# A new order for the first sequence's steps, its sums in the tiles of the weights

## The chip, the cores and the metric

The kernel runs on one core of one Trainium2 chip. The metric is the device time of one execution in microseconds (us), the median of several; lower is better.

## What is computed

A batch of two sequences (3008 x 256 each) goes through a circular convolution along the sequence, done as an FFT, a product with a filter and an inverse FFT, and then through two dense layers with their own activations:

```python
X = np.fft.rfft(x, axis=1)
y = np.fft.irfft(X * (filt_r + 1j * filt_i), n=3008, axis=1)   # 2 x 3008 x 256
h = y.reshape(6016, 256) @ moe_w_in                            # 256 -> 2048
g = np.where(h > 0, h, np.exp(np.minimum(h, 0)) - 1)
z = g @ moe_w_out                                              # 2048 -> 256
h = z @ moe2_w_in
out = (h * np.clip(h + 3, 0, 6) / 6) @ moe2_w_out
```

## The kernel before

3008 is 47 x 64, so each transform is done as two stages of small matrix products. The 256 channels are worked as two halves h = 0, 1. For the first sequence a half goes through these steps, each named by a letter, the half and a number in a string of tokens, `PROLOGUE`, which is walked once in order (line 1042). Each token issues its instructions on the engines' queues, and every engine works its queue strictly in that order.

- **A** (`s1t`): first stage, seven groups of up to five products; one copy of the bank into the tile `zt` (line 79 on ScalarE, line 81 on VectorE). Those of half 0 are done ahead of the string.
- **T** (`tr`): four transposes (line 173) and one copy, six per half. **S** (`s2_mm`, then `mult`): the second stage's product (line 204), then on VectorE three products with the filter, straight from PSUM (line 216 twice on 64 rows, line 217 once), and on GpSimd one sum of the two results into a tile `ws` (line 219).
- **F** (`f_sign`, line 149): GpSimd changes signs in the imaginary part of one filter tile, once it is loaded. `mult` of the same (h, g) needs it. Two are issued ahead of the string, ten by tokens.
- **I** (`i2_mm`, `i2_evac`): the inverse second stage's product from `ws` (line 224), a ScalarE copy (line 234), a store to DRAM (line 235). **V**: four loads of a half's stores (line 239). **O** and **o** (`i1_mm`, `i1_evac`): the inverse first stage (line 247) with its copies on ScalarE (O) or VectorE (o).
- **x, b, M, B** load, split and transform the beginning of the second sequence's half 0 (its first stage, lines 88 to 90 with the tile `s_h`); **X** splits results into high and low parts (lines 84 and 85); **G** and **H** are the first products of the first dense layer.
- **w** loads a weight tile; **c** and **k** make one step each in the conversion of weights: seven steps for the first tile (c), twelve for the next ones (k). The steps are: |w| on ScalarE (line 297), two scalings on VectorE (lines 299, 300), one each of lines 304, 306 and 308 on VectorE, a ScalarE copy with the difference of line 316, and the sum of line 318. The first k of a tile also issues the load of a raw tile two tiles on.

After the string a loop over units of the first layer follows, whose VectorE work per unit is line 500, line 85 and further conversion steps.

All loads and stores named here are issued by SyncE in the order of the program; the filter tiles are loaded ahead of the string, in an order of their own (`LOADS`). A PSUM bank (seven rotate) is given to the next product that asks, in the order in which the banks are given up, so step n waits for the copy or the products of the step seven places ahead of it. In SBUF, tiles of 2 KB per partition come from `p2` (20 of them), the weights' tiles from `wpool` (16 of 4 KB).

Of the kernel before, what the change touches and what calls it, by code (L numbers as in the profile page):

```python
# [9 lines left out]
F32 = mybir.dt.float32  # L10
# [13 lines left out]
P = 128  # L24
# [23 lines left out]
def fft_conv_moe_moe2(ctx, tc, xp, fq, sg, cs1, cs1t, cs2, ci2, ci1, ident, w1i, w1o, w2i, w2o, out):  # L48
    nc = tc.nc
    const = ctx.enter_context(tc.tile_pool(name="const", bufs=1))  # L50
    wpool = ctx.enter_context(tc.tile_pool(name="wpool", bufs=16))
# [9 lines left out]
    def name(s):  # L61
        uid[0] += 1
        return f"{s}_{uid[0]}"
# [4 lines left out]
    def t2(shape, dt=F32):  # L68
        return p2.tile(shape, dt, tag="t2", name=name("t2"))

    def bank():
        return ps.tile([P, 512], F32, tag="ps", name=name("ps"))
# [4 lines left out]
    def evac(eng, dst, src):  # L77
        if eng is nc.scalar:
            nc.scalar.activation(dst, src, AF.Copy)
        else:  # L80
            eng.tensor_copy(dst, src)  # L81
# [10 lines left out]
    def flat(t):  # L92
        return t.rearrange("p k d -> p (k d)")
# [4 lines left out]
    def sorted_(t, k=2):  # L98
        return t.rearrange("p (b a) -> p a b", a=k)
# [13 lines left out]
    def load_mat(key, src, queue=nc.scalar):  # L113
        k, m = src.shape
        mats[key] = const.tile([k, m], F32, name=key)
        queue.dma_start(mats[key], src)
# [17 lines left out]
    xin, filt, zs, ws, vin, accs, yblk = {}, {}, {}, {}, {}, {}, {}  # L134
# [7 lines left out]
    def f_load(b, h, g):  # L142
        filt[b, h, g] = t4([P, 2, 4, P])
        nc.sync.dma_start(filt[b, h, g], fq[h, g])
# [9 lines left out]
    def s1t(b, h, jg, eng):  # L154
        if jg == 0:
            zt[h] = p12.tile([P, NK2, 2, 2, NJ], F32, tag="zt", name=name("zt"))
        acc = bank()
        j0, n = jg * TG, min(TG, NJ - jg * TG)
        for j in range(j0, j0 + n):
            nc.tensor.matmul(  # L160
                acc[:, (j - j0) * KP : (j - j0 + 1) * KP], xin[b, h, j // 8][:KP, j % 8, :],
                mats["s1t"][:KP], start=True, stop=True,
            )
        evac(
            eng,
            zt[h].rearrange("p k c h j -> p (c h) k j")[:, :, :, j0 : j0 + n],
            acc[:, : n * KP].rearrange("p (j c k) -> p c k j", j=n, c=4),
        )

    def tr(b, h, g, eng):  # L170
        acc = bank()
        for k in range(4):
            nc.tensor.transpose(
                acc[:, k * P : (k + 1) * P],
                zt[h][:, 4 * g + k].rearrange("p c h j -> p (c h j)"), mats["id"],
            )
        zs[b, h, g] = t2([P, 512])
        evac(eng, zs[b, h, g], acc)
# [29 lines left out]
    def mult(b, h, g):  # L208
        f = filt.pop((b, h, g))
        acc, parted = accs.pop((h, g)), lambda t: t  # L210
        if b:
            acc, parted = sorted_(acc), halves_of
        u, v = t2([P, 512]), t2([P, 512])
        for c in range(2):
            a, o = slice(64 * c, 64 * c + 64), slice(64 - 64 * c, 128 - 64 * c)
            nc.vector.tensor_tensor(out=parted(v[o]), in0=acc[a], in1=parted(flat(f[a, 1])), op=ALU.mult)
        nc.vector.tensor_tensor(out=parted(u), in0=acc, in1=parted(flat(f[:, 0])), op=ALU.mult)
        ws[b, h, g] = t2([P, 512])
        nc.gpsimd.tensor_tensor(out=ws[b, h, g], in0=u, in1=v, op=ALU.add)

    def i2_mm(b, h, g, parts=None):
# [622 lines left out]
    def fetch1(f):  # L844
# [9 lines left out]


    PROLOGUE = """
        T00 T01 T02 S00 T03 F01 S01 T04 F01 S02 T05 F01 S03 I00 F01 S04 I01 F01 A10 A11 F01
        S05 I02 A12 A13 A14 I03 F01 A15 A16 I04 T10 c01 T11 c01 w00 I05 F01 x00 x01 V00 T12
        S10 T13 S11 T14 F01 S12 T15 S13 I10 F01 S14 I11 S15 I12 O00 I13 b00 c01 O01 I14 c01
        b01 o02 O03 I15 M00 c01 b02 V10 c01 X00 O04 w01 b03 c01 X01 k02 O05 O06 X02 k02 B00  # L860
        B01 B02 B03 G00 G01 k03 O10 o11 G02 X10 o12 X11 O13 X12 o14 k02 H00 H01 k02 O15 k01
        H02 O16
    """
    LOADS = [(0, None, q, None) for q in range(4)]
    for x in "F00 F01 F02 F03 X0 X1 X2 X3 F04 F05 F10 W0 M F11 F12 F13 F14 F15".split():
# [150 lines left out]
    with tc.manual_schedule():  # L1016
        for key, src in (("s1t", cs1t), ("id", ident), ("sg", sg), ("s2", cs2), ("i2", ci2), ("i1", ci1)):
            load_mat(key, src)
        three = const.tile([P, 1], F32, name="three")
        nc.vector.memset(three, 3.0)  # L1020
        engs = (nc.scalar, nc.vector)

        acc = bank()
        for n in WARM:
            zeros = (nc.const_aps.tensor(0.0, [P, k], F32) for k in (P, n))
            nc.tensor.matmul(acc[:, :n], *zeros, start=True, stop=True)
        for h, g, q, r in LOADS:
            if q is not None:
                x_load(0, h, q)
            elif g is not None:  # L1030
                f_load(0, h, g)
            elif r is not None:
                w_raw(0, r)
            else:
                load_mat("s1", cs1, nc.sync)
        for jg in range(JG):
            s1t(0, 0, jg, engs[jg % 2])
        lead = w_chain(0, WLEAD, lambda f: None)
        f_sign(0, 0, 0)
        f_sign(0, 0, 1)  # L1040
        nsign = 2
        for step in PROLOGUE.split():
            what, h, g = step[:-2], int(step[-2]), int(step[-1])
            if what == "T":
                tr(0, h, g, nc.scalar if g > 1 else engs[g])
            elif what == "S":
                s2_mm(0, h, g)
                mult(0, h, g)
            elif what == "A":
                s1t(0, h, g, engs[g % 2])  # L1050
            elif what == "I":
                i2_mm(0, h, g)
                i2_evac(0, h, g)
            elif what == "V":
                for q in range(4):
                    v_load(0, h, q)
            elif what == "O":
                i1_mm(0, h, g)
                i1_evac(0, h, g, nc.scalar)
            elif what == "o":  # L1060
                i1_mm(0, h, g)
                i1_evac(0, h, g, nc.vector)
            elif what == "k":
                steps(conv, g)
            elif what == "c":
                steps(lead, g)
            elif what == "X":
                x_split(0, g, h)
            elif what == "F":
                for _ in range(g):  # L1070
                    f_sign(0, *divmod(nsign, 6))
                    nsign += 1
            elif what == "x":
                x_load(1, h, g)
            elif what == "w":
                w_raw(0, WLEAD + g)
            elif what == "b":
                s1_split(h, g)
            elif what == "B":
                s1_mm(1, h, g, parts.pop(("x", h, g)))  # L1080
                s1_evac(1, h, g)
            elif what == "G":
                g1_half(units[g], 0)
            elif what == "H":
                g1(units[g])
                if g:
                    g_split(units[g - 1])
            elif what == "M":
                split_mat("s1")

        for n, u in enumerate(units):
            place[0] = n
            for fn in pre[n]:
                fn()
            if n >= NI:
                g1(u)
                g_split(units[n - 1])
            if n >= SKEW:
                g2(units[n - SKEW])
            for fn in post[n]:  # L1100
                fn()
        def rest(n):
            def run():
                if n == NU:
                    g_split(units[-1])
                g2(units[n - SKEW])
                for fn in post[n]:
                    fn()
            return run

        old = None
        n = place[0] = NU
        for l, p in ROUNDS:
            for q in range(GROUPS):
                old = group(l, p, q, old, [rest(NU + i) for i in range(3)], pre[n : n + 4])
                n += 4
        prod(old.l, old.p, old.q, 3, old.c, False)
        old.high((1, 1))
        old.gate((1, 0))
        old.add((0, 1), old.u2, old.c)  # L1120
        old.low((1, 1))
        old.high((1, 0))
        old.relu((0, 1))
        old.low((1, 0))
        old.gate((0, 1))
        old.high((0, 1))
        old.low((0, 1))
        for key in ((0, 0), (1, 1), (1, 0), (0, 1)):
            old.second(key)
            if key == (1, 0):  # L1130
                out_evac(old.l, old.p, 0)
        out_evac(old.l, old.p, 1, True)
# [82 lines left out]
```

## Time and profile before

| | us |
|---|---|
| median of 3 runs | 1050.47 (1050.16 to 1052.39) |
| the profiled execution | 1050.34 |
| its span, first to last instruction | 1048.6 |
| PE busy | 1037.6 |
| VectorE (DVE) busy | 876.6 |
| ScalarE (ACT) busy | 807.0 |
| GpSimd (POOL) busy | 198.6 |

The span is cut by the profile into rows of instructions with start, duration and the idle time ahead of them. PE is the matrix engine, PEld its weight loads, SPq the issues of SyncE. The ends of matrix products are modelled, so the times between starts tell more than the busy share: a product of lines 204 and 224 takes 0.86 between starts (two instructions), a group of ten on lines 160 or 247 takes 1.11, and one product of lines 88 to 90 with 512 columns takes 0.216.

### The profile page before, as it was taken

The numbers are of one execution on the slowest core, as the hardware profiler recorded it, in microseconds if no ns is written. First come the engines' busy times: TensorE is split into PE (matmuls) and PEld (weight loads), VectorE is DVE, ScalarE is ACT, GpSimd is POOL, SyncE is SP. The second block draws the span as 40 slices with busy tenths as digits, with TensorE's granted clock in tenths as the row PEclk, the third lists the DMA queues.
The fourth block names the chain that finished last, engine by engine and source line by source line (L and its number), as shares of the span: only waits on it lengthen the run. The fifth ranks groups of instructions, "written<-read, shape, count | busy, mean of one in ns | idle before, by whom it ended". The sixth has DMA issues, their size and how long they took to land.

```text
span 1048.6 us, 14397 instructions
## 1 busy us (share of the span) xinstructions
PE 1037.6 (99%) x5022; PEld 913.1 (87%) x5022; DVE 876.6 (84%) x1412; ACT 807.0 (77%) x1453; POOL 198.6 (19%) x215
## 2 busy tenths in 40 slices
PE   8999999999999999999999999999999999999998
PEld 6688888888899889988888888888888888888998
DVE  4799999788877988788988988888888888887776
ACT  3488887897788888888988877777777777777766
POOL 3700001355437943200111100010010010000000
PEclk9999999999999999999999999999999999999999
DMA  9983100475536634510474531100100100100101
GB/s 263 330 280 124 46 1 1 143 228 176 167 125 213 220 128 141 178 41 1 161 261 132 209 121 41 41 21 21 41 21 21 41 18 18 41 1 1 41 1 36
DMA packets 58057, 107.32 MB, mean 102 GB/s; under 512 B 5024, under 2 KB 33696, under 8 KB 57984
## 3 DMA queue, kind: packets, MB, share of 16 engines
q1 hardware_dynamic: 52112, 88.16, 25.2%
q0 software_dynamic: 4896, 17.83, 5.2%
q8 instruction: 39, 0.64, 0.2%
q10 hardware_dynamic: 976, 0.41, 0.2%
q14 instruction: 34, 0.28, 0.1%
HBM read 69.42 MB, written 36.96 MB: 101 GB/s over the span
## 4 chain that ended last, share of the span: by engine, by line
PE 87%; DMA 4%; POOL 3%; DVE 2%; ACT 2%; issue 1%; ACTq 0%; SPq 0%; POOLq 0%; DVEq 0%
PE ps L88 26%; PE ps L90 26%; PE ps L89 26%; PE lone L90 3%; PE lone L88 3%; PE lone L89 3%; DMA t<-in_fq 2%; DMA scr<-t 1%; PE ps L247 1%; POOL t L367 1%; PE ps L224 1%; POOL t L377 1%; DMA sg<-in_sg 1%; POOL t L332 1%; POOL t L356 0%
## 5 line engine op out<-in xcount | busy, mean ns | idle before, releaser
L88 PE MATMUL ps<-t,w 128*128 128x512 f32 (+1 forms) x1072 | 403.0, 376 | 0.9 <-DVE t L500 0.8
L90 PE MATMUL ps<-t,w 128*128 128x512 f32 (+1 forms) x1072 | 401.8, 375 | 0.1
L89 PE MATMUL ps<-t,w 128*128 128x512 f32 (+1 forms) x1072 | 401.6, 375 | 0.2 <-DVE w L318 0.2
L88 PEld LDWEIGHTS ps<-t,w 128*128 128x128 f32 x1072 | 202.6, 189 | 25.6 <-DVE t L500 2.0
L90 PEld LDWEIGHTS ps<-t,w 128*128 128x128 f32 x1072 | 202.6, 189 | 25.3 <-DVE t L692 1.3
L89 PEld LDWEIGHTS ps<-t,w 128*128 128x128 f32 x1072 | 202.6, 189 | 24.9 <-DVE w L318 1.6
L692 DVE TENSOR_TENSOR t<-t,t 128x512 fp32r<-128x512 f32 (+1 forms) x256 | 175.7, 700 | 25.8 <-ACT t L687 24.3
L687 ACT ACTIVATE t<-t 128x512 fp32r<-128x512 f32 (+1 forms) x256 | 154.3, 616 | 6.4 <-DVE t L677 6.1
L641 ACT ACTIVATE t<-ps 128x512 f32<-128x512 f32 (+1 forms) x175 | 102.5, 586 | 61.5 <-PE ps L90 59.8
L661 ACT ACTIVATE t<-t,three 128x512 f32<-128x512 f32 (+1 forms) x143 | 96.5, 707 | 38.6 <-DVE t L647 37.9
L677 DVE SCALAR_TENSOR_TENSOR t<-t,t 128x512 f32<-128x512 f32 (+1 forms) x143 | 96.8, 703 | 33.3 <-ACT t L661 32.8
L497 ACT ACTIVATE t<-ps 128x512 f32<-128x512 f32 (+1 forms) x128 | 74.3, 580 | 46.9 <-PE ps L90 36.4
L647 DVE TENSOR_TENSOR t<-ps,t 128x512 f32<-128x512 f32 (+1 forms) x128 | 86.6, 677 | 11.5 <-ACT t L641 11.0
L498 ACT ACTIVATE t<-t 128x512 f32<-128x512 f32 (+1 forms) x128 | 79.3, 620 | 4.0
L500 DVE SCALAR_TENSOR_TENSOR ps<-t,ps 128x512 f32<-128x512 f32 (+1 forms) x76 | 50.4, 663 | 28.4 <-ACT t L498 27.9
L85 DVE TENSOR_TENSOR t<-t,t 128x512 fp32r<-128x512 f32 (+2 forms) x96 | 69.9, 733 | 4.2 <-ACT t L84 4.1
L84 ACT ACTIVATE t<-t 128x512 fp32r<-128x512 f32 (+2 forms) x108 | 65.2, 616 | 2.5 <-DVE t L81 2.0
L561 POOL TENSOR_TENSOR t<-t,t 128x512 f32<-128x512 f32 (+1 forms) x12 | 16.2, 1351 | 253.2 <-DVE t L647 224.0
L88 PE MATMUL ps<-t,t 128*128 128x512 f32 (+1 forms) x160 | 60.1, 376 | 0.0
L89 PE MATMUL ps<-t,t 128*128 128x512 f32 (+1 forms) x160 | 60.1, 376 | 0.0
L90 PE MATMUL ps<-t,t 128*128 128x512 f32 (+1 forms) x160 | 60.1, 376 | 0.0
L90 PE MATMUL lone<-t,w 128*128 128x512 f32 (+1 forms) x144 | 54.0, 375 | 1.0 <-DVE t L85 1.0
(118 smaller groups left out, 1612.3 us busy)
## 6 DMA issues: line engine op xcount, KB each, us to landing
t<-in_fq SPq DMA_DIRECT2D x24, 512.0 KB, 6.2
scrw<-t SPq DMA_DIRECT2D x16, 512.0 KB, 3.0
w<-scrw POOLq DMA_DIRECT2D x16, 512.0 KB, 4.3
scr<-t SPq DMA_DIRECT2D x24, 256.0 KB, 3.4
t<-scr SPq DMA_DIRECT2D x16, 384.0 KB, 5.1
t<-in_xp SPq DMA_DIRECT2D x15, 384.0 KB, 6.3
scrx<-t SPq DMA_DIRECT2D x10, 512.0 KB, 3.0
t<-scr POOLq DMA_DIRECT2D x10, 512.0 KB, 5.9
```

The costliest lines, as they stand in the source:

```text
L85: eng.tensor_tensor(out=lo, in0=src, in1=_f32(hi), op=ALU.subtract)
L88: nc.tensor.matmul(acc, wh, xh, start=start, stop=False, skip_group_check=more)
L89: nc.tensor.matmul(acc, wl, xh, start=False, stop=False, skip_group_check=more)
L90: nc.tensor.matmul(acc, wh, xl, start=False, stop=stop, skip_group_check=more)
L497: nc.scalar.activation(r, acc, AF.Relu, scale=-1.0)
L498: nc.scalar.activation(t[:, :n], t[:, :n], AF.Exp, scale=-1.0)
L641: nc.scalar.activation(like(t, self.n), got(bank_, self.n), AF.Copy)
L647: nc.vector.tensor_tensor(out=like(self.h[key], n), in0=got(bank_, n), in1=like(u, n), op=ALU.add)
L661: nc.scalar.activation(like(r, n), h, AF.Relu, bias=three)
L677: stt(out=r, in0=r, scalar=6.0, in1=h, op0=ALU.min, op1=ALU.mult)
L687: nc.scalar.activation(gh[:, : self.n], g[:, : self.n], AF.Copy)
L692: nc.vector.tensor_tensor(out=gl[:, :n], in0=g[:, :n], in1=_f32(gh[:, :n]), op=ALU.subtract)
```

## The change

The string `PROLOGUE` is written anew: all six S of half 0 now stand ahead of I00, and all six S of half 1 ahead of I10; the A of half 1 are spread among the S and I of half 0; the sign changes stand elsewhere (ten, as before), and so do the conversion steps: five of the seven c stand ahead of S10, and the twelve k end at O11. All copies of half 1's A steps are on ScalarE; of the T copies the first is on VectorE and the others on ScalarE. The sums `ws` of the first sequence lie in a half of a weights' tile.

```diff
-        ws[b, h, g] = t2([P, 512])
+        ws[b, h, g] = t2([P, 512]) if b else wpool.tile([P, 2, 512], F32, tag="w", name=name("ws"))[:, 0]
...
-        T00 T01 T02 S00 T03 F01 S01 T04 F01 S02 T05 F01 S03 I00 F01 S04 I01 F01 A10 A11 F01
-        S05 I02 A12 A13 A14 I03 F01 A15 A16 I04 T10 c01 T11 c01 w00 I05 F01 x00 x01 V00 T12
-        S10 T13 S11 T14 F01 S12 T15 S13 I10 F01 S14 I11 S15 I12 O00 I13 b00 c01 O01 I14 c01
-        b01 o02 O03 I15 M00 c01 b02 V10 c01 X00 O04 w01 b03 c01 X01 k02 O05 O06 X02 k02 B00
-        B01 B02 B03 G00 G01 k03 O10 o11 G02 X10 o12 X11 O13 X12 o14 k02 H00 H01 k02 O15 k01
-        H02 O16
+        F01 T00 T01 T02 S00 F01 T03 T04 S01 S02 F01 S03 w00 T05 A10 F01 A11 S04 S05 I00 A12 c01
+        I01 c01 c01 c01 F01 F01 A13 A14 A15 A16 I02 F01 T10 c01 T11 I03 F01 S10 T12 F01 S11 I04
+        I05 T13 S12 x00 T14 F01 T15 S13 S14 S15 x01 k01 V00 I10 b00 b01 k01 I11 c01 I12 M00 b02
+        I13 O00 O01 I14 X00 c01 O02 k01 O03 I15 X01 b03 O04 k01 w01 k01 B00 V10 B01 X02 B02 k01
+        G00 O05 k01 B03 o06 k01 k01 k01 G01 k01 G02 O10 O11 k01 X10 O12 X11 o13 H00 X12 o14 H01
+        O15 o16 H02
...
-                tr(0, h, g, nc.scalar if g > 1 else engs[g])
+                tr(0, h, g, nc.scalar if h or g else nc.vector)
...
-                s1t(0, h, g, engs[g % 2])
+                s1t(0, h, g, nc.scalar)
```

## Rows read from the trace of the kernel before

**Rows 1.** The page: busy time by engine; granted clock and GB/s in 40 slices.
```profile
PE 1037.6 (99%) x5022; PEld 913.1 (87%) x5022; DVE 876.6 (84%) x1412; ACT 807.0 (77%) x1453; POOL 198.6 (19%) x215
...
PEclk9999999999999999999999999999999999999999
...
GB/s 263 330 280 124 46 1 1 143 228 176 167 125 213 220 128 141 178 41 1 161 261 132 209 121 41 41 21 21 41 21 21 41 18 18 41 1 1 41 1 36
```
**Rows 2.** Timeline of PE: start, duration, what, idle before it.
```profile
27.54 1.25 PE L160 MATMUL ps<-s1t,t 96*128 96x96 f32 x10
29.53 2.47 PE L160 MATMUL ps<-s1t,t 96*128 96x96 f32 x20 [0.74 <-DVE t L217]
...
53.74 1.05 PE L224 MATMUL ps<-t,i 128*128 128x512 f32 x2
...
60.96 0.38 PE L90 MATMUL ps<-t,w 128*128 128x512 f32 x1
61.91 2.44 PE L247 MATMUL ps<-i,t 96*128 96x94 f32 x20 [0.58 <-DMA t<-scr]
...
79.49 0.38 PE L90 MATMUL ps<-t,w 128*128 128x512 f32 x1
80.65 0.48 PE L88 MATMUL ps<-t,w 128*128 128x512 f32 x1 [0.78 <-DVE t L500]
```
**Rows 3.** Waits of PE, 14 to 90 us, one line: total, times, longest.
```profile
PE ps L224 <- POOL t L219: 0.6, 3, 0.2
```
**Rows 4.** Timeline of POOL, the first sequence.
```profile
26.29 1.04 POOL L149 TENSOR_TENSOR t<-t,sg 128x512 f32<-128x512 f32 x1 [1.47 <-DMA t<-in_fq]
...
51.55 1.60 POOL L219 TENSOR_TENSOR t<-t,t 128x512 f32<-128x512 f32 x1 [1.04 <-DVE t L217]
```
**Rows 5.** Timeline of DVE, the first sequence.
```profile
27.36 1.39 DVE L216 TENSOR_TENSOR t<-ps,t 64x512 f32<-64x512 f32 x2 [1.67 <-POOL t L149]
...
31.50 0.69 DVE L217 TENSOR_TENSOR t<-ps,t 128x512 f32<-128x512 f32 x1
...
38.44 1.39 DVE L216 TENSOR_TENSOR t<-ps,t 64x512 f32<-64x512 f32 x2 [0.51 <-PE ps L204]
...
51.93 1.78 DVE L304 SCALAR_TENSOR_TENSOR t<-raw,t 128x512 uint32<-128x512 uint32 x1
```
**Rows 6.** Source L273, the first weight tile's second load alone (issued at 19.4).
```profile
DMA to landing us min/median/max: 10.9/10.9/10.9
```
**Rows 7.** Timeline of ACT: one |w| step; four copies in a row.
```profile
36.34 0.66 ACT L297 ACTIVATE t<-raw 128x512 f32<-128x512 f32 x1
...
60.41 2.08 ACT L190 ACTIVATE t<-ps 96x512 f32<-96x512 f32 x4
```
**Rows 8.** Groups of DVE by line, 14 to 72 us: count, busy, mean ns.
```profile
L308 DVE SCALAR_TENSOR_TENSOR t<-raw,t 128x512 f32<-128x512 uint32 x2 | 1.4, 688 | 0.0
...
L300 DVE TENSOR_SCALAR t<-t 128x512 uint32<-128x512 uint32 x3 | 1.3, 427 | 0.1
```
**Rows 9.** Timeline of DVE and POOL, 233 to 235 us, where both want SBUF.
```profile
233.07 0.61 DVE L299 TENSOR_SCALAR t<-t 128x512 f32<-128x512 f32 x1
...
233.34 1.24 POOL L149 TENSOR_TENSOR t<-t,sg 128x512 f32<-128x512 f32 x1
...
233.79 1.07 DVE L300 TENSOR_SCALAR t<-t 128x512 uint32<-128x512 uint32 x1
```
**Rows 10.** Timeline of SP: the loads of half 0 and of half 1.
```profile
43.21 1.72 SPq L239 DMA_DIRECT2D t<-scr  x4
...
57.85 1.73 SPq L239 DMA_DIRECT2D t<-scr  x4
```
**Rows 11.** Timeline of DVE ahead of PE's wait at 80 us.
```profile
72.74 0.82 DVE L304 SCALAR_TENSOR_TENSOR t<-raw,t 128x512 uint32<-128x512 uint32 x1
...
74.05 0.84 DVE L308 SCALAR_TENSOR_TENSOR t<-raw,t 128x512 f32<-128x512 uint32 x1
...
79.89 0.70 DVE L500 SCALAR_TENSOR_TENSOR t<-t,ps 128x512 f32<-128x512 f32 x1
```

## The prediction

> **What bounds the kernel now.** I read the page first: PE is busy 99% of the span and its granted clock stands in the top tenth in all forty slices, while VectorE, the next engine, is at 84% [rows 1]. So time can come only from moments in which PE waits, or be lost by making new ones. A busy share hides short waits, so I went on to the starts of PE's instructions. Behind 82 us the instructions and their order stay as they are. Up to 14.3 us, where half 0's first T starts, PE waits for the first loads, which stay too. Between the two, four kinds of waits can be won:
>
> - A13 should start at 27.54 + 1.11 = 28.65 and starts at 29.53: 0.88, for VectorE's line 217 [rows 2]. It needs the bank that S04, seven places ahead, gives up.
> - Three I steps wait for GpSimd's sum, 0.6 in all [rows 3].
> - O10 should start at 60.96 + 0.22 = 61.18 and starts at 61.91: 0.73, for the loads of half 1's stores [rows 2].
> - A product of the first layer should start at 79.49 + 0.22 = 79.71 and starts at 80.65: 0.94, for VectorE's line 500 [rows 2].
>
> That is 3.15 us, 0.3% of the time. PE's own work is the same before and after: no product is added or removed.
>
> **Half 0.** The order of loads is unchanged and its filter tiles arrive as before. The sign change for S04 starts at 26.29, having waited for its tile [rows 4], and S04's products run from 27.36 [rows 5]; the new order has the same GpSimd sequence here (change for S04, a sum, change for S05), so I keep these times. What moves is what PE does meanwhile. By 0.86 for each S and I, 0.44 for each T and 1.11 for each A, from 14.3 us on the new order is through with A14 at 29.7. A15 takes the bank of S04, free at 29.5: no wait. A16 takes the bank of S05. Today S05's products end at 31.50 + 0.69 = 32.19 [rows 5], begun behind a copy that VectorE no longer makes; the sign change ends 0.4 earlier, so they end at 31.75. PE waits for A16 from 30.8 to 31.78: 0.98, in place of the 0.88 for A13.
>
> **ScalarE.** It gets three more copies (A11, A13, A15, some 0.6 each) and T01, T11, and gives T00 away; VectorE loses them. ScalarE has room, but c1 now stands behind A12's copy. It reads the first raw weight tile, whose second load lands at 19.4 + 10.9 = 30.3 [rows 6]. ScalarE reaches c1 at 27.4 and stands until 30.3, with the copies of I01 and A13 to A16 queued behind. With |w| at 0.66 and 0.52 for each copy in a row [rows 7], A16's copy ends at 33.3, and T10, which needs it, starts at 33.4: 0.3 of wait after I02. T10, T11, I03 and S10 take 2.6, so S10's product ends at 36.0.
>
> **VectorE against GpSimd: where the gain of half 1 goes.** From 36.1 VectorE could begin S10's products, 2.3 us earlier than today's 38.44 [rows 5]. But c2 to c5 (lines 299, 300 and 306 at 0.43, lines 304 and 308 at 0.69, together 2.7 [rows 8]) now stand between S05 and S10, at 31.75, and GpSimd works there without pause: the sum of S05 and the sign changes for S10 to S13, all of them loaded. The rows show what two such neighbours do to each other. Line 304, which is 308's like, took 1.78 beside a sum at 51.55 [rows 4, 5]; it ended 0.55 after the sum did. At 233 us line 299, a sign change and line 300 go one after the other: line 300 took 1.07 and ended 0.28 after the sign change [rows 9]. The products of S, which read PSUM, keep 0.69 beside GpSimd. So c2 to c5 alternate with the sum (1.27) and three sign changes (1.04 each): 31.75 + 0.4, +1.2, +0.3, +0.9, +0.65, +0.9, +0.3, +0.9, +0.65 = 38.0. S10's products start at 38.0, 0.44 ahead of today instead of 2.3.
>
> The Trainium skill says in "SBUF — State Buffer", section "Who interferes with whom", that the shared port pair is an exclusive lock, held for a whole instruction, and that the loser fully blocks. By that rule each of the nine pieces counts with its full duration, S10 starts at 38.75, and everything below comes 0.75 later, about 1050.0 in all. The row at 233 us shows the order of the rule but not the full duration: a blocked instruction has part of its way behind it when its neighbour ends (0.28 of 0.43).
>
> From S10 on VectorE gives up one bank each 2.13 (1.39, 0.69 and 0.05 between [rows 5]), so S11 ends at 42.25, S12 at 44.4, S15 at 50.85. PE, working on without a wait, is through T15 at 41.2; S13 takes S11's bank and waits 1.05. I10 and I11 follow without wait; I13 waits for its sum, which stands behind the last sign change, until 48.05 (0.55). O00 then starts at 48.9, O01 at 50.0, I14 (bank of S15) at 51.1, O02, O03, and I15 starts at 54.2. Today I15 starts at 53.74 [rows 2]. So PE arrives 0.45 **late** with the same work behind it. The three waits of 0.6 are gone, but the two for S13 and I13 cost 1.6.
>
> **The loads in between.** Those of half 0's stores (line 239) go out at 43.21 today [rows 10]; I05, whose store they wait for, does not come earlier in the new order, since it ends at 39.1 behind the same filter loads. Half 1's are of use 61.91 - 57.85 = 4.06 after their issue [rows 2, 10]. In the new order a pair of weight loads stands ahead of each of the two (k1 issues one, w01 is moved ahead of V10): 512 KB, 1.6 at 330 GB/s [rows 1]. Half 0's are then there at 43.21 + 4.06 + 1.6 = 48.9, just when O00 wants them; half 1's pair goes out while SyncE still waits for I15's store (4.1 from I15's start to the issue). I count nothing for both; the upper bound is 1.6 each. For half 1, O10 starts today 61.91 - 53.74 = 8.17 after I15 [rows 2], the copy, the store, its landing and the load in a row. That gives 62.35. PE has 7.2 of other work between I15's end and O10 (O04 to o06, four B, and now all three G instead of two), so it is there at 62.25: the wait shrinks from 0.73 to 0.1, a gain of 0.62.
>
> **The conversion after that.** From 72.74 to 74.89 VectorE does steps k10 to k12 (lines 304, 306, 308), 2.1 us, and the line 500 that PE waits for comes at 79.89 [rows 11], in a row of VectorE's work that is unbroken from there to here. In the new order all twelve k are through by O11, in a stretch where VectorE waits today for splits. With 2.1 us less before it that line 500 is no longer late: gain 0.94. Bounds: nothing, if ScalarE instead is late with the exponentials ahead of line 500, and 0.94.
>
> **Without cost.** The sums in the weights' tiles: twelve of sixteen are taken for them, the first weight tile is taken behind S15, and the fourth and later weights, which come to tiles of sums again, are converted when all I steps are long done. At most a copy of line 314 would wait there. T00's copy on VectorE (0.69 for 0.60) delays S00 by 0.1, ahead of a VectorE that has until 27.36 to wait anyway.
>
> **Sum**, against the profiled execution's 1050.34 (the median is 0.13 above it): +0.45 - 0.62 - 0.94 = -1.1, so 1049.2.
>
> **Rivals.**
> - *No contention* (27%): GpSimd and VectorE don't hinder each other at c2 to c5, for instance because GpSimd's instructions come later than I think. S10 starts with its product at 36.1, S13 waits for nothing, I15 starts at 52.95. Then -0.8 - 0.62 - 0.94: 1048.0. For it: line 299 lost only 0.18 beside the sign change. Against: what line 300 lost [rows 9].
> - *The wait at 80 us stays* (12%): another thing than k10 to k12 makes line 500 late. Then +0.45 - 0.62: 1050.1. Against it stands VectorE's unbroken row of work from 72 us.
> - *Slower: S10 late* (21%). Each 1 us by which S10's products start later goes one to one to the banks of S13, I11 and I14, and so to I15 and O10. If GpSimd comes first in every turn (the sum and four sign changes, 5.4, and 2.7 of VectorE's), S10 starts at 39.9, and the sum is 1051.1. It decides from S10 at 39.1: there the gain is used up. For it: five GpSimd instructions stand ready at 31.8. Against: line 299 stands right behind S05's products on VectorE's own queue, and the sum must first be told of their end.
>
> The forecast has the remaining 40%. A measurement of this kernel can tell about 0.2%, 2.1 us, so faster means below 1048.4 and slower above 1052.6. Most of the contention-free case and a fifth of the forecast's own spread are faster: 0.30. Slower needs the last rival and more: 0.08. The range is 1047.2 (contention-free and the 0.98 or 1.05 wait shorter) to 1051.6 (the slower case with the loads for O10 late); the forecast's own is 1048.4 to 1050.0.
>
> **What would show it.** Right: A16 follows S05's products with about 1 us of idle PE; lines 299 to 308 stretched to about 1 us each between 31.7 and 38.5; S10's first line 216 near 38; S13 with a wait for line 217; O10 almost without; no wait of PE at 75 to 82 us. Wrong: line 216 of S10 near 36 (no contention) or after 39.1 (slower), a copy of an A step that waits on ScalarE beyond 33.5, or a wait for loads at O00.

## The result, and the profile after

The changed kernel takes 1055.24 us (median of 5 runs, 1050.35 to 1064.13), the kernel before 1050.16 beside it (5 runs, 1048.48 to 1052.39): 1.0063 times the time, interval 1.0039 to 1.0086. The forecast was 1049.2, with a range up to 1051.6. The kernel is slower, by 5 us, and its runs spread over 14.

The profiled execution was the fastest of the five, 1050.35 us, and looks like the one before. The page's busy times and granted clock, against [rows 1]:

```profile
PE 1037.9 (99%) x5022; PEld 913.3 (87%) x5022; DVE 877.2 (84%) x1406; ACT 810.0 (77%) x1459; POOL 200.6 (19%) x215
...
PEclk9999999999999999999999999999999999999999
```

PE's timeline, against [rows 2] (start, duration, what, idle before it):

```profile
26.57 3.93 PE L160 MATMUL ps<-s1t,t 96*128 96x96 f32 x34
...
45.41 1.13 PE L224 MATMUL ps<-ws,i 128*128 128x512 f32 x2 [1.08 <-POOL ws L219]
47.48 2.44 PE L247 MATMUL ps<-i,t 96*128 96x94 f32 x20 [0.94 <-DMA t<-scr]
...
61.95 4.23 PE L247 MATMUL ps<-i,t 96*128 96x94 f32 x36 [0.89 <-DMA t<-scr]
...
78.67 0.38 PE L90 MATMUL ps<-t,w 128*128 128x512 f32 x1
79.09 0.48 PE L88 MATMUL ps<-t,w 128*128 128x512 f32 x1
```

A13 to A16 now run in one row, without the wait of 0.88; line 500's wait near 80 us has shrunk from 0.94 to 79.09 - 78.67 - 0.22 = 0.2. New are 1.08 ahead of I13 and 0.94 ahead of O00, only one I step apart, and O10 waits for its loads longer than before, 0.89 against 0.58. Counted from the first T (13.50 here, 14.32 before) to the same product of the first layer (at 100.35 here, 101.91 before), the changed kernel needs 86.85 us and the one before 87.58: 0.7 gained, of a forecast 1.1.

So this execution doesn't hold the 5 us. The list of runs does: mean granted clock and time go together.

| executions of the changed kernel | us | mean granted clock |
|---|---|---|
| the profiled one | 1050.35 | 0.999 |
| the other four | 1054.42, 1055.24, 1058.82, 1064.13 | 0.997, 0.996, 0.992, 0.988 |

What a clock short of full costs can be worked out: 0.992 lacks 0.008, which is 8.4 us of 1050, and that run is 8.5 above the profiled one; for the other three it gives 3.2, 4.2 and 12.6, against 4.1, 4.9 and 13.8. Most of the loss goes with TensorE's clock. Where it falls is not to be seen in a trace in which it didn't; hence the first experiment is the kernel itself.

### The profile page after: what moved, and what is told of

Same layout as the page of the kernel before. It is cut to its first block, busy times and chain, and to the rows that moved or that the text cites. A ratio compares the mean times of both kernels' runs of the same rounds, so it can differ in the third digit from the quotient of the medians.

```text
span 1048.6 us, 14394 instructions
## 1 busy us (share of the span) xinstructions
PE 1037.9 (99%) x5022; PEld 913.3 (87%) x5022; DVE 877.2 (84%) x1406; ACT 810.0 (77%) x1459; POOL 200.6 (19%) x215
## 4 chain that ended last, share of the span: by engine, by line
PE 93%; DVE 3%; DMA 2%; ACT 2%; issue 0%; DVEq 0%; SPq 0%; ACTq 0%
PE ps L90 26%; PE ps L88 26%; PE ps L89 26%; PE lone L90 3%; PE lone L88 3%; PE lone L89 3%; PE ps L247 2%; PE ps L160 1%; DMA t<-scr 1%; PE ps L204 1%; PE ps L224 1%; DMA scr<-t 0%; PE ps L1026 0%; PE ps L173 0%; DVE t L85 0%
## 5 line engine op out<-in xcount | busy, mean ns | idle before, releaser
L641 ACT ACTIVATE t<-ps 128x512 f32<-128x512 f32 (+1 forms) x175 | 102.6, 586 | 61.3 <-PE ps L90 59.7
```

Of the source, the lines that this page charges most:

```text
L641: nc.scalar.activation(like(t, self.n), got(bank_, self.n), AF.Copy)
```

## Experiments

Three groups of runs, each with runs of the kernel before on the same chip: its medians there were 1050.07 (23 runs), 1049.41 (35) and 1049.90 (17). The first group holds the first three rows and "loads first", the second the two half fillings, "loads first, with zeros" and the mended order, the third the rest; each had another chip. A ratio with its 95% interval is the record's, of a kernel against the kernel before beside it, and not the quotient of the two medians. "Fallen" counts the executions with a mean granted clock below 0.999; the kernel before has 5 of 75.

| kernel | us, median | ratio, interval | fallen |
|---|---|---|---|
| changed, again | 1055.31 | 1.0053 (1.0039 to 1.0067) | 6 of 6 |
| old order, new tiles | 1051.36 | 1.0013 (1.0004 to 1.0022) | 0 of 11 |
| zeros in all three pauses | 1050.21 | 1.0011 (1.0000 to 1.0021) | 3 of 12 |
| zeros in half 0's pauses | 1051.50 | 1.0032 (1.0011 to 1.0053) | 4 of 12 |
| zeros in half 1's pause | 1053.31 | 1.0040 (1.0025 to 1.0055) | 9 of 12 |
| loads first | 1059.87 | 1.0106 (1.0091 to 1.0121) | 5 of 5 |
| loads first, with zeros | 1051.42 | 1.0008 (0.9993 to 1.0024) | 0 of 11 |
| mended order | 1051.12 | 1.0018 (1.0008 to 1.0028) | 1 of 11 |
| before, with a longer pause | 1059.34 | 1.0082 (1.0061 to 1.0102) | 6 of 6 |
| zeros, conversion late | 1050.89 | 1.0015 (0.9994 to 1.0035) | 3 of 10 |

With the two single executions below and the five above, the changed kernel itself has fallen in 11 of 13 executions.

**The changed kernel again, and two single executions of it.** No edit.

> The changed kernel once more. Theory A: in some executions PE's granted clock falls to its lower level somewhere in or behind the first sequence, because PE now pauses twice close together (I13 waits 1.1 us for GpSimd's sum, O00 0.9 us for the loads, with one product between), and the time is lost one to one with the clock. Then the times spread again, from about 1050 to 1060 or more, median 1053 to 1057, each run's time above 1050 equal to (1 - mean clock) x 1050 within about 1 us, while the kernel before, run beside it, stays within 1048 to 1053 at a mean clock of 0.998 or more. Theory B: the spread was the chip's state in that hour and belongs to neither kernel. Then both spread alike, or neither does, and the two medians lie within 2 us.

> The changed kernel as it is, one more profiled execution, to see where the granted clock falls. Theory: a stretch at half the clock starts behind I13 and O00 (near 49 to 56 us) or behind O10 (near 63 us), and the time above 1050 is near 1050 times what the mean clock lacks to 1. Rival: the time is above 1052 with the clock full throughout, or the clock falls in a stretch that the change does not touch.

> As the run before this one, once more: the same kernel, the same theory and rival; two executions tell whether the place of the fall is the same each time.

Again, the six executions took 1052.43 to 1058.49 at mean clocks of 0.992 to 0.998, while the 23 of the kernel before beside them took 1051.83 or less at 0.999 or above: the loss belongs to the kernel.

The two single executions are the cleanest pair of the study: same kernel, same chip, 1055.16 and 1051.34. PE's timeline of the first:

```profile
46.53 1.12 PE L224 MATMUL ps<-ws,i 128*128 128x512 f32 x2 [1.07 <-POOL ws L219]
48.84 4.52 PE L247 MATMUL ps<-i,t 96*128 96x94 f32 x20 [1.19 <-DMA t<-scr]
53.15 1.97 PE L224 MATMUL ps<-ws,i 128*128 128x512 f32 x2
```

and of the second:

```profile
46.43 1.13 PE L224 MATMUL ps<-ws,i 128*128 128x512 f32 x2 [1.07 <-POOL ws L219]
48.87 2.44 PE L247 MATMUL ps<-i,t 96*128 96x94 f32 x20 [1.31 <-DMA t<-scr]
51.15 1.05 PE L224 MATMUL ps<-ws,i 128*128 128x512 f32 x2
```

The pauses are the same to 0.12 us, and behind them the same twenty products take 4.52 in the one and 2.44 in the other. The windows say why (from:to, length, busy time of each engine, then PEclk, DMA share, GB/s); the first execution:

```profile
45.00:48.50 3.50, 1.58 (x4) 0.30 (x2) 3.38 (x6) 3.05 (x6) 2.70 (x3) 1.00 1.07 283
48.50:56.00 7.50, 7.16 (x29) 6.16 (x30) 5.42 (x10) 2.03 (x5) 1.68 (x2) 0.54 0.95 253
56.00:62.00 6.00, 6.00 (x39) 5.02 (x39) 4.06 (x7) 4.93 (x13) 0.00 (x0) 1.00 0.48 134
```

and the second:

```profile
48.50:56.00 7.50, 7.13 (x53) 6.21 (x53) 7.14 (x13) 4.19 (x11) 1.65 (x1) 1.00 1.03 283
```

Read the PEclk column, not PE's busy time: 7.16 and 7.13 are alike, but 29 products against 53. In the first execution the granted clock went to its lower level (1.2 instead of 2.4 GHz) from 48.88 to 55.71, right behind the two pauses. Half of these 6.83 us is 3.4; the runs differ by 3.8. The Trainium skill, "TensorE: Matmul & The Clock Gate", section "Terms", prices time at the lower clock in the same way, and the trace agrees.

The profiled run of the first group (1058.49) fell twice, at 55.35 for 3.41 us, behind I13 and a wait of 2.00 at O00, and earlier, in a place that the change doesn't touch:

```profile
10.16 6.43 PE L160 MATMUL ps<-s1t,t 96*128 96x96 f32 x32 [1.56 <-DMA t<-in_xp]
```

That is the wait for the first loads; the clock was low from 10.98 to 21.22. The old order with a longer pause, below, shows a fall in the same place, so this one is not put down to the change. It is the larger part of this execution's loss: half of 10.24 is 5.1, and half of 3.41 is 1.7, of 8.4 above the median of before.

**The old order with the new tiles.** The string is that of before; the sums stay in the weights' tiles.

```diff
-        ws[b, h, g] = t2([P, 512])
+        ws[b, h, g] = t2([P, 512]) if b else wpool.tile([P, 2, 512], F32, tag="w", name=name("ws"))[:, 0]
```

> The order and the engines of before, only the sums of the first sequence in the tiles of the weights. Both theories expect 1050 within 1.5 us and no spread of its own under A; if the tiles themselves do harm (a third theory, C: the address of the sums or the pool's waits), it spreads or slows like the changed kernel.

1051.36 and no fall in 11. The tiles cost 1.3 us (1.0004 to 1.0022); the falls come with the order and its choice of engines. This kernel has a pause at O00 too, but a single one, with an O10 as before:

```profile
44.47 1.12 PE L224 MATMUL ps<-ws,i 128*128 128x512 f32 x2 [0.24 <-POOL ws L219]
46.70 1.32 PE L247 MATMUL ps<-i,t 96*128 96x94 f32 x10 [1.11 <-DMA t<-scr]
...
61.16 2.44 PE L247 MATMUL ps<-i,t 96*128 96x94 f32 x20 [0.63 <-DMA t<-scr]
```

These rows are PE's timeline. In this trace 1.11 by itself did not let the clock fall; the changed kernel has as much twice, with one I step between.

**Zeros in the pauses.** Products of zeros, two instructions of 128x512 that nobody reads, keep PE at work where it would wait. They are added work.

```diff
-        I13 O00 O01 I14 ...
+        Z01 I13 Z01 O00 O01 I14 ...
-        ... G01 k01 G02 O10 O11 ...
+        ... G01 k01 G02 Z01 O10 O11 ...
+            elif what == "Z":
+                pad = lone()
+                for _ in range(g):
+                    zeros = (nc.const_aps.tensor(0.0, [P, k], F32) for k in (P, 512))
+                    nc.tensor.matmul(pad, *zeros, start=True, stop=True)
```

> The changed kernel with three added products of zeros on PE (0.86 us each, into a bank that nothing reads then), ahead of I13, of O00 and of O10, where PE pauses. They add no wait for the steps behind them beyond some 0.2 us each. Theory A: the clock does not fall any more, or less often; the times draw together at 1049 to 1051.5 although work was added. Theory B: nothing changes against the changed kernel beside it, or it is 0 to 1 us slower. A rival within A, that products of zeros don't count for the clock, would also leave the spread.

The two edits apart, first the upper line of the diff alone, then the lower:

> The changed kernel with products of zeros ahead of I13 and O00 alone (0.86 us each). Theory A1: the pair of pauses at 44 to 47.5 us lets the clock fall; then this kernel is as calm as the one with three fillings, median 1049.5 to 1051, at most one run in six above 1053. Theory A2: the pause ahead of O10 does it (1.05 us, followed by 44 steps with 96 columns); then it spreads like the changed kernel, median 1053 to 1057.

> The changed kernel with one product of zeros ahead of O10 alone. A1: spreads like the changed kernel, median 1053 to 1057, and its trace has the clock fall between 46 and 60 us. A2: calm, median 1049.5 to 1051. If both this and the other are half calm, both pauses take part.

More work makes the kernel faster: from 1055.31 to 1050.21, with 9 of 12 executions at full clock instead of none of six. With the pause ahead of O10 left, 4 of 12 fell, three of them deep (1056.87, 1057.78, 1062.17); with those of I13 and O00 left, 9 of 12, six of them at 0.997 or 0.998. The latter's profiled execution (1053.62) was low from 48.94 to 55.77, right behind I13 and O00, as the first single execution was:

```profile
48.50:56.00 7.50, 7.29 (x30) 6.28 (x31) 5.07 (x9) 2.30 (x5) 1.64 (x1) 0.54 0.91 243
```

So the pauses of I13 and O00 take part. That O10's does is not shown: 9 of 12 can't be told from the 11 of 13 of the changed kernel, and no trace of its order falls behind O10. Nor does a step of zeros always fill its pause: with those of half 0 alone, O00 still waited 1.16 in the profiled execution (1049.96, at full clock).

**Loads first.** My first mend moved half 0's loads (V00) ahead of the x and weight loads, and O00 ahead of I13.

```diff
-        I05 T13 S12 x00 T14 F01 T15 S13 S14 S15 x01 k01 V00 I10 b00 b01 k01 I11 c01 I12 M00 b02
-        I13 O00 O01 I14 X00 c01 O02 k01 O03 I15 X01 b03 O04 k01 w01 k01 B00 V10 B01 X02 B02 k01
+        I05 T13 S12 T14 F01 T15 S13 S14 S15 V00 x00 x01 I10 I11 k01 I12 c01 O00 M00 I13 O01 k01
+        c01 O02 I14 b00 b01 X00 O03 I15 b02 k01 X01 b03 O04 k01 w01 k01 B00 V10 B01 X02 B02 k01
```

> The changed kernel with the loads of half 0's stores ahead of the two loads of the second sequence and of the weight pair, and O00 to O02 ahead of I13 and I14, so that PE has work where it paused from 44 to 47.5 us. Theory A: both pauses there go (2.3 us), the clock does not fall, and the time is 1047.5 to 1049.5 without spread. Theory B: 2 us less than the changed kernel in each state, the spread stays. If the loads are late for another reason than the queue, O00 waits as before.

A miss: 10 us slower than before, all five executions fallen. The pauses at 45 to 48 us are gone as meant but for 0.29, and PE is early, but half 1's loads don't come earlier with it (issued at 58.97; 57.27 in the changed kernel's profiled run). PE's timeline:

```profile
45.29 1.32 PE L247 MATMUL ps<-i,t 96*128 96x94 f32 x10 [0.29 <-DMA t<-scr]
...
62.95 8.32 PE L247 MATMUL ps<-i,t 96*128 96x94 f32 x40 [2.66 <-DMA t<-scr]
70.97 0.77 PE L88 MATMUL ps<-t,w 128*128 128x512 f32 x1
71.54 0.63 PE L89 MATMUL ps<-t,w 128*128 128x512 f32 x1
...
80.76 0.38 PE L90 MATMUL ps<-t,w 128*128 128x512 f32 x1
```

Three small pauses became one of 2.66 (2.8 between starts), and behind it forty products take 8.32 instead of some 4.7, and a product of line 89 takes 0.63 instead of 0.38. The windows show that PE is never idle in that time and yet low until 80.57:

```profile
62.00:68.00 6.00, 5.05 (x26) 5.08 (x27) 1.65 (x3) 1.53 (x4) 0.00 (x0) 0.63 0.96 305
68.00:75.00 7.00, 7.00 (x31) 6.64 (x31) 3.17 (x6) 3.06 (x7) 0.00 (x0) 0.50 1.07 372
75.00:83.00 8.00, 8.00 (x33) 7.16 (x32) 3.78 (x8) 5.02 (x10) 0.00 (x0) 0.65 1.07 366
```

**Loads first, with zeros ahead of O10.** The same kernel with one step more, three products of zeros in that pause.

```diff
-        ... G01 k01 G02 O10 O11 ...
+        ... G01 k01 G02 Z03 O10 O11 ...
```

> The order with the loads of half 0 first, whose clock fell at 63.5 us behind a pause of 2.8 us ahead of O10, with three products of zeros (2.6 us) in that pause. If the pause lets the clock fall, it stays up, and 17 us at half clock (8.5 us) come back: 1050 to 1052 instead of 1059.9. If something else in this order does it (the steps of 96 columns themselves, or the bunching of loads), it stays at 1058 to 1061.

PE's timeline and the windows of the same stretches:

```profile
61.69 2.75 PE L1094 MATMUL lone<-const-float32-0.0 128*128 128x512 f32 x6
64.28 1.92 PE L247 MATMUL ps<-i,t 96*128 96x94 f32 x16
```

```profile
62.00:68.00 6.00, 6.00 (x40) 4.67 (x39) 3.24 (x8) 2.03 (x7) 0.00 (x0) 1.00 0.97 285
68.00:75.00 7.00, 7.00 (x49) 6.57 (x49) 5.37 (x12) 6.25 (x14) 0.00 (x0) 1.00 0.96 327
```

O10 starts 1.3 us later than without the zeros, and the kernel is 1059.87 - 1051.42 = 8.45 us faster, or 7.8 with each counted from the median of before beside it (9.80 and 2.01 above). The stretch that was low lasted 17.07 us; half of it is 8.5, less the 1.3 it is 7.2. Of the two traces, counted from the first T, the one with zeros is 6.7 us ahead at about 100 us and 7.9 at the end; the rest comes near 550 us, where only the one without zeros has waits (see "The sum at full clock"). The same narrow products follow the zeros at full clock, so they alone don't bring the fall.

**The kernel before, with a longer pause.** If pauses do it, the old order must lose too. One step moved: V10, half 1's loads, behind two pairs of weight loads.

```diff
-        b01 o02 O03 I15 M00 c01 b02 V10 c01 X00 O04 w01 b03 c01 X01 k02 O05 O06 X02 k02 B00
+        b01 o02 O03 I15 M00 c01 b02 c01 X00 O04 w01 b03 c01 X01 k02 V10 O05 O06 X02 k02 B00
```

> The old order with one thing moved: V10, half 1's loads, stands behind two pairs of weight loads (k02, w01) instead of ahead of them, so that O10's wait grows from 0.73 us to some 2 or more. Everything else is the kernel before. Theory (a longer pause ahead of O10 lets TensorE's granted clock fall behind it, whatever the order of the steps): the profile shows O10 with a wait of 2 us or more; the mean granted clock is 0.996 or less in most runs and the median is 1054 or more. Rival (the new order does something else that makes the clock fall, and a pause alone costs its own length): the clock stays at 0.999 or above and the median is 1051 to 1052.

1059.34, all six fallen. PE's timeline and windows, against the 0.58 at O10 of [rows 2]:

```profile
64.40 0.38 PE L90 MATMUL ps<-t,w 128*128 128x512 f32 x1
67.80 3.82 PE L247 MATMUL ps<-i,t 96*128 96x94 f32 x20 [3.02 <-DMA t<-scr]
71.33 0.77 PE L88 MATMUL ps<-t,w 128*128 128x512 f32 x1
```

```profile
68.00:75.00 7.00, 7.00 (x34) 6.73 (x34) 1.41 (x3) 1.19 (x2) 0.00 (x0) 0.54 1.03 338
75.00:83.00 8.00, 8.00 (x37) 7.46 (x37) 4.25 (x9) 4.57 (x9) 0.00 (x0) 0.55 0.97 328
```

The pause is 67.80 - 64.40 - 0.22 = 3.2 between starts where it was 0.73, so 2.4 more; the median rose by 9.4. The clock was low from 68.61 to 82.26 in this trace, 13.65 us; half of that and the 2.4 make 9.2. It was low early as well, from 10.58 to 20.82, behind the first loads, which this edit doesn't touch: half of all 23.9 and the 2.4 make 14.3, and the profiled run stands 13.6 above the median of before.

**The mended order.** V00 first, V10 and I15's copy ahead of the second sequence's splits, the last k steps late, and two products of zeros ahead of O10. These lines stand in place of the changed kernel's last four; `Z` is as above.

```diff
+        I05 T13 S12 T14 F01 T15 S13 S14 S15 V00 x00 x01 I10 I11 I12 c01 O00 M00 I13 O01 c01 O02
+        I14 X00 O03 I15 V10 b00 b01 X01 b02 b03 O04 w01 k02 O05 B00 B01 X02 k02 B02 B03 G00 k02
+        o06 G01 k01 G02 Z02 O10 O11 X10 O12 X11 o13 H00 X12 k02 o14 H01 k02 O15 k01 o16 H02
```

> The loads of half 0 first, the loads of half 1 and the splits of the second sequence ordered so that ScalarE takes I15's copy ahead of them, five of the twelve conversion steps at their old places, and two products of zeros ahead of O10. PE should reach O10 near 60 and find its loads at 61.3, 0.6 to 1.2 us ahead of the kernel before; with the clock up throughout: 1048 to 1050. If the clock falls behind O10 in spite of the filling: above 1053.

A miss too: 1051.12 where 1048 to 1050 was expected, with one fall in 11. The clock is kept, but nothing is won over the kernel before. O10's loads were expected at 61.3; it starts at 62.55 in the profiled execution.

**The conversion steps late.** Zeros in all three pauses, and c2 to c5 behind S15 instead of ahead of S10, to price what VectorE and GpSimd cost each other there.

```diff
-        I01 c01 c01 c01 F01 F01 A13 A14 A15 A16 I02 F01 T10 c01 T11 I03 F01 S10 T12 F01 S11 I04
-        I05 T13 S12 x00 T14 F01 T15 S13 S14 S15 x01 k01 V00 ...
+        I01 F01 F01 A13 A14 A15 A16 I02 F01 T10 T11 I03 F01 S10 T12 F01 S11 I04
+        I05 T13 S12 x00 T14 F01 T15 S13 S14 S15 c01 c01 c01 c01 x01 k01 V00 ...
```

> The changed kernel with products of zeros in its three pauses (added work, 128x512, as in the earlier run with three), and with the conversion steps c2 to c5 of the first weight tile moved from behind I01 to behind S15. If c2 to c5, stretched beside GpSimd, are what holds S10 back, as I forecast, S10's first line 216 starts at the end of S05's products and its own sign change, 1.5 us or more earlier than in the changed kernel (33.9 or less against 35.4), and S15's line 217 ends earlier by the same. If S10 waits for its filter tile or sign change in any case, it moves by less than 0.5 us. The time: at full clock 1049 to 1051 by either.

First the changed kernel, VectorE's timeline and one row of GpSimd's:

```profile
28.87 0.69 DVE L217 TENSOR_TENSOR t<-ps,t 128x512 f32<-128x512 f32 x1
29.47 0.42 DVE L299 TENSOR_SCALAR t<-t 128x512 f32<-128x512 f32 x1
29.93 1.38 DVE L300 TENSOR_SCALAR t<-t 128x512 uint32<-128x512 uint32 x1
31.34 1.41 DVE L304 SCALAR_TENSOR_TENSOR t<-raw,t 128x512 uint32<-128x512 uint32 x1
32.79 1.15 DVE L306 TENSOR_SCALAR t<-t 128x512 uint32<-128x512 uint32 x1
33.97 1.41 DVE L308 SCALAR_TENSOR_TENSOR t<-raw,t 128x512 f32<-128x512 uint32 x1
35.41 1.39 DVE L216 TENSOR_TENSOR t<-ps,t 64x512 f32<-64x512 f32 x2
```

```profile
30.98 5.29 POOL L149 TENSOR_TENSOR t<-t,sg 128x512 f32<-128x512 f32 x4
```

then this kernel, VectorE and PE:

```profile
30.84 0.69 DVE L217 TENSOR_TENSOR t<-ps,t 128x512 f32<-128x512 f32 x1
36.01 1.39 DVE L216 TENSOR_TENSOR t<-ps,t 64x512 f32<-64x512 f32 x2 [4.47 <-POOL t L149]
```

```profile
33.10 1.09 PE L173 MATMUL ps<-id,zt 128*128 128x128 f32 x8 [0.33 <-ACT zt L79]
34.03 1.02 PE L224 MATMUL ps<-ws,i 128*128 128x512 f32 x2
34.89 1.02 PE L204 MATMUL ps<-t,s 128*128 128x512 f32 x2
```

The expected 33.9 was missed: S10's products start at 36.01. But this execution's loads came later (the raw weight tile at 30.17 instead of 28.19), so the distance from the end of S05's products counts: 36.01 - 31.53 = 4.48 here, 35.41 - 29.56 = 5.85 in the changed kernel. There S10's own product was ready at 32.97 + 1.02 = 33.99 and VectorE came 1.42 later, straight from line 308; here VectorE stands free and waits until S10's product ends, at 35.91 (34.89 + 1.02). (The row names GpSimd's line 149, but S10's own sign change is the first of four that run from 32.84 in a row, and long done.) So c2 to c5 hold S10 back by 1.4. At full clock the seven runs give 1049.5 to 1051.7, like the kernel with zeros alone (1049.35 to 1051.4): 1.4 us at S10 are not to be seen in the end.

## Why the prediction was wrong

**The step that failed is the first one**: "So time can come only from moments in which PE waits, or be lost by making new ones." It took the length of a pause for its price. The page showed a granted clock in the top tenth in all slices [rows 1], and I counted every later product at that clock, whatever pauses the new order put ahead of it. A term for the clock was missing from the sum and from all rivals; the slowest of them came to 1051.1. The runs show what stands in its place: behind 1.1 + 1.2 of pause, 6.83 us at half the clock (the first single execution); behind 2.8 or 3.2 in one piece, 17.07 and 13.65, and all 11 executions of those two kernels fell. Filling the 2.8 with idle work took 7.8 us back, counted from the kernel before; lengthening the pause in the old order lost 9.4.

**The loads in between** supplied the pauses at O00 and O10; "a wait for loads at O00" was one of my signs of being wrong. I counted nothing for half 0's loads, with 1.6 as a bound. They go out earlier than before, at 40.49 instead of 43.21 [rows 10], but behind the two x loads and a pair of weight loads just issued, and the first lands 6.8 later, where I had reckoned 4.06 + 1.6 to their use. In "loads first", where they go ahead of both, the first landed after 3.9. PE is ready for O00 at 46.5 and waits until 47.48; the other traces of the same kernel show 1.19, 1.31 and 2.00. SyncE's rows of the changed kernel:

```profile
39.18 0.42 SPq L269 DMA_DIRECT2D raw<-in_w1i  x1
39.65 0.46 SPq L273 DMA_DIRECT2D raw<-in_w1o  x1
40.49 2.01 SPq L239 DMA_DIRECT2D t<-scr  x4
```

For O10 I had 0.1 left of the 0.73 between starts; it was 1.04 in the profiled run (0.89 of idle), and 0.49 of idle in the second single execution. I13 waited 0.73 to 1.08 for GpSimd's sum, against 0.55.

**Half 0 and ScalarE**: A16 should wait 0.98 and T10 0.3. In the profiled run neither waits, with loads about 2 us earlier than before. T10 waited 0.31 to 0.36 for a copy on ScalarE in four traces where the raw weight tile came at 28.97 to 30.17, as forecast for 30.3. A16 waited in none: with the conversion late, where S05's products ended at 31.53, it ran on, and I02 behind it waited 0.39 for them. Nor did S13 wait its 1.05: in the profiled run it starts at 39.01, before line 217 of S11 ends at 39.65. So neither took the bank that I had counted to it.

**VectorE against GpSimd** was right: the four lines behind line 299 stretched to 1.15 to 1.41 each, GpSimd's four sign changes to 5.29 instead of 4.04 (with the conversion late), and 5.85 from S05's end to S10's start, where I had 6.25. S10's start itself, 35.41, is near the 36 that I had set as the sign of no contention: S05's products ended at 29.56 instead of 31.75, so only the distance tells. The full blocking that the page "SBUF — State Buffer" of the Trainium skill ("Who interferes with whom") describes would have been 7.0; the trace doesn't bear it out. Counted at S10 the price is 1.4, I had 1.9.

**The wait at 80 us** went almost whole, 0.74 of 0.94, as forecast. The rival with S10 late is out: S10 came earlier than before, and the slower result has another cause.

**The sum at full clock.** 0.7 were gained up to 100 us, of 1.1. Between 545 and 560 us the profiled run then lost 1.3 against the one before, with short waits for VectorE that the kernel before doesn't have there. PE's waits of the changed kernel, 500 to 600 us (total, times, longest):

```profile
PE ps L90 <- DVE t L692: 0.3, 1, 0.3
PE ps L88 <- DVE t L647: 0.3, 1, 0.3
```

All six traces of a kernel with the new tiles and without zeros lose 1.0 to 1.7 there, the old order among them (1.5, about what its median is slower); the six traces with zeros lose at most 0.2, and so does the old order with its old tiles and a longer pause. So a second step failed: under "Without cost" I put the tiles at nothing, and with the old order they cost 1.3. How they bring these waits about, and why added zeros take them away, I didn't settle; part of what the zeros win in the experiments is this, and not the clock.

**What stays open.** Which execution falls can't be told from the pauses: the two single executions have the same ones. Three of 12 executions fell with zeros in all three pauses; no trace shows where. And in the third group the kernel before fell in 4 of 17 executions, in the others in 1 of 58. Those four stand 3.5 to 4.7 above their median, about what an early fall behind the first loads costs (5.1); no trace of them exists, so that this is what they were is not shown.

## What to carry to other kernels

On a kernel that PE bounds, price a new pause of PE by what it may do to the granted clock as well as by its length. Be wary of two pauses close together; that the pair does what neither would alone is suggested here, not shown, since no run filled only one of the two. List the pauses that a new order makes, with the work between them, and look at the mean clock of several runs: one profile at full clock says nothing about the others. If a pause can't be avoided, idle products in it are a cheap test. Here they took most of the loss away, but no kernel of this study beat the one before.

## What the runs showed of the hardware

- The lower clock held on while PE was busy: in "loads first" from 63.51 to 80.57, with PE's row full from 62.95 on. The products of that time are largely the narrow ones of line 247 (94 columns), beside some of 512.
- Products of zeros kept the clock up: 0.999 or above in all 11 executions of "loads first, with zeros", in none of five without.
- VectorE and GpSimd slow each other in both directions: four sign changes took 5.29 us beside c2 to c5 and 4.04 without them, the lines 300 to 308 of the conversion 1.15 to 1.41 against 0.43 to 0.69 [rows 8].
